# A chunked attention head pair: values and row sums from one product [V | 1] on half the rows of the array

## The chip, the cores and the metric

The kernel runs on one core of a Trainium2 chip. Times are device microseconds (us) of an execution. The kernel before takes 293.57 us (median of 4 executions beside the changed kernel, 292.65 to 294.11).

Engine names in the profile: PE is TensorE (matmuls), PEld its weight loads, DVE is VectorE, ACT is ScalarE, POOL is GpSimd, SP is SyncE, which issues transfers.

## The reference

Attention inside chunks of 64 tokens, then a two-layer network with a leaky ReLU (slope 0.01) on all 4608 tokens:

```python
# q, k, v: (8, 8, 576, 64) = batch, heads, tokens, head size
scores = scale * q_c @ k_c.T            # 64 x 64 in each chunk
attn   = exp(scores - max) ; attn /= sum(attn)
out    = attn @ v_c
x      = out as (4608 tokens, 512)
h      = x @ w_in                       # 512 -> 2048
y      = max(0.01 * h, h) @ w_out       # 2048 -> 512
```

## The kernel before

The kernel works in nine blocks (j) of 512 tokens. While TensorE does the network of block j, the attention of block j+1 is threaded between its steps. Two heads form a pair (kk), with one head in partitions 0 to 63 and the other in 64 to 127; a block has four pairs, so there are 36 pairs in all. Each pair passes four stages:

```python
def attn_t(j, kk, n=0):      # keys into a block-diagonal tile kd, 64 rows each
    ...
    for hh in range(2):
        ...
        if hh == 0 and (j == 0 and kk < 3 or j >= NPT and n >= NFC):
            nc.scalar.activation(out=dst, in_=src, func=AFT.Copy, ...)
        else:
            nc.vector.tensor_copy(out=dst, in_=src)     # the "kd copies"

def attn_s(j, kk):           # scores: 8 matmuls of 64 columns, then e = exp
    ...
def attn_x(j, kk):
    e = live[j, kk]
    zp = psum([128, TB], FP32, "zp", "at")
    nc.tensor.matmul(out=zp, lhsT=onesd, rhs=e, start=True, stop=True)   # sums
    xp = psum([128, R, 128], FP32, "xp", "at")
    for c in range(NC):                                                  # values
        nc.tensor.matmul(out=xp[:, :, c * NI:(c + 1) * NI],
                         lhsT=VD[j % NVD][:, kk, c, :, :],    # block diagonal, zeros off it
                         rhs=e[:, :, c * NI:(c + 1) * NI], start=True, stop=True)
    rz = sbuf([128, TB], FP32, "rz", 2)
    nc.scalar.activation(out=rz, in_=zp, func=AFT.Ln, ...)
    nc.scalar.activation(out=rz, in_=rz, func=AFT.Exp, ..., scale=-1.0)  # 1/sum
    live[j, kk] = (xp, rz)

def attn_n(j, kk):           # the "multiply"
    ...
    nc.vector.tensor_tensor(out=xT[j][:, kk, :], in0=xp..., in1=rz, op=ALU.mult)
```

The loop of block j has 32 steps n: 16 for the first layer (`hp`, four accumulating matmuls each, one per pair of xT), then the second (`mp`, sums of products with w_out, which VectorE combines). From block 3 on, pair kk does `attn_t` at step 7kk, `attn_s` at 7kk+3, `attn_x` at 7kk+5 and `attn_n` at 7kk+7. So step 7 holds the multiply of pair 0 **and** the kd copies of pair 1, and the loop issues the later stage first:

```python
def regular(first, gap, lags=(0, 3, 5, 7)):
    return [[first + gap * kk + lag for kk in range(NKK)] for lag in lags]
...
for s in (3, 2, 1, 0):                       # attn_n before attn_x, attn_s, attn_t
    for kk in range(NKK):
        at.setdefault(steps[s][kk], []).append((STEPS[s], kk))
```

PSUM, the memory that matmuls write into, has four banks for attention tiles (`at`) and four for the network (`mm`).

The softmax here doesn't subtract the row's maximum and nothing guards it: scores larger than these inputs give would overflow.

Of the kernel before, what the change touches and what calls it, by code (L numbers as in the profile page):

```python
# [9 lines left out]
FP32 = mybir.dt.float32  # L10
ALU = mybir.AluOpType
AFT = mybir.ActivationFunctionType
# [3 lines left out]
def kernel(  # L16
# [9 lines left out]
    nc = tc.nc  # L26
# [5 lines left out]
    CH = 64  # L32
    NKK = H // 2
    NFC = d_ff // 128
    TB = 512
    NJ = n_tok // TB
    NC = TB // CH
    R = 4
    NI = CH // R
# [11 lines left out]
    onesd = sb.tile([128, 128], FP16, name="onesd")  # L51
# [9 lines left out]
    NVD = 2  # L61
    KD = [sb.tile([128, NC, 2, CH], FP16, name=f"kd{m}") for m in range(NKD)]
    VD = [sb.tile([128, NKK, NC, 2, CH], FP16, name=f"vd{m}") for m in range(NVD)]
# [1 line left out]
        nc.vector.memset(t[0:64, :, 1, :], 0.0)  # L65
        nc.vector.memset(t[64:128, :, 0, :], 0.0)

    def clear_vd(m, eng):
        eng.memset(VD[m][0:64, :, :, 1, :], 0.0)
        eng.memset(VD[m][64:128, :, :, 0, :], 0.0)  # L70

    clear_vd(0, nc.vector)

    w_in = sb.tile([128, NKK, d_ff], FP16, name="w_in")
    w_out = sb.tile([128, NFC, d_model], FP16, name="w_out")
# [20 lines left out]
    def sbuf(shape, dtype, name, bufs):  # L96
        return sb.tile(shape, dtype, name=name, tag=name, bufs=bufs)

    def psum(shape, dtype, name, tag):
        return ps.tile(shape, dtype, name=name, tag=tag, bufs=4)  # L100


    def alloc(j):
        raw[j] = (
            sbuf([128, H, R * D], FP32, "qf", 2),
            sbuf([128, H, R * D], FP32, "kf", 2),
            sbuf([128, len(HW), NC, D], FP32, "vf", 2),
        )
        half[j] = tuple(sbuf([128, NKK, R, 2, D], FP16, n, 2) for n in ("qh", "kh"))
# [109 lines left out]

    def attn_x(j, kk):  # L220

        e = live[j, kk]
        zp = psum([128, TB], FP32, "zp", "at")
        nc.tensor.matmul(out=zp, lhsT=onesd, rhs=e, start=True, stop=True)  # L224
        xp = psum([128, R, 128], FP32, "xp", "at")
        for c in range(NC):
            nc.tensor.matmul(  # L227
                out=xp[:, :, c * NI:(c + 1) * NI],
                lhsT=VD[j % NVD][:, kk, c, :, :],
                rhs=e[:, :, c * NI:(c + 1) * NI],  # L230
                start=True,
                stop=True,
            )
        rz = sbuf([128, TB], FP32, "rz", 2)
        nc.scalar.activation(out=rz, in_=zp, func=AFT.Ln, bias=0.0, scale=1.0)  # L235
        nc.scalar.activation(out=rz, in_=rz, func=AFT.Exp, bias=0.0, scale=-1.0)  # L236
        live[j, kk] = (xp, rz)

    def attn_n(j, kk):

        if j not in xT:
            xT[j] = sbuf([128, NKK, TB], FP16, "xT", 2)
        xp, rz = live.pop((j, kk))
        nc.vector.tensor_tensor(  # L244
            out=xT[j][:, kk, :], in0=xp.rearrange("p r t -> p (r t)"), in1=rz, op=ALU.mult
        )

    STEPS = (attn_t, attn_s, attn_x, attn_n)

    def mm1_part(j, hp, fc, kk):  # L250
# [8 lines left out]
    def mm1_end(j, hp, fc):  # L259
        if fc == 0:  # L260
            gT[j] = sbuf([128, NFC, TB], FP16, "gT", 1)
        nc.scalar.activation(  # L262
            out=gT[j][:, fc, :], in_=hp, func=AFT.Prelu, bias=0.0, scale=1.0, alpha=0.01
        )
# [144 lines left out]
    with tc.manual_schedule():  # L409
# [9 lines left out]
        for step in range(NKK + 2):  # L419
            if step < NKK:  # L420
                if step == 3:
                    w_dma.append(load_w_in(0))
                cast_qk(1, 0, step, nc.gpsimd)
                cast_qk(0, 0, step, nc.gpsimd if step else nc.vector)
                if step == 3:
                    cast_v(0, 2)
                    w_dma.append(load_w_in(1))
                    cast_v(0, 3)
                    w_dma += [load_w_in(g) for g in range(2, 4)]
            p = step - 2  # L430
            if 0 <= p < NKK:
                attn_x(0, p)
            p = step - 1
            if 0 <= p < NKK:
                attn_s(0, p)
            if step < NKK:
                attn_t(0, step)
            p = step - 2
            if 0 <= p < NKK:
                attn_n(0, p)  # L440
            if step < NKK:
                keep_warm(3)
# [3 lines left out]
                mm1_part(0, hp, fc, kk)  # L446
        for fc, hp in enumerate(hps):
            mm1_end(0, hp, fc)
        clear_vd(1, nc.vector)
        alloc(1)  # L450
        for kk in range(NKK):
            first = load_qk(1, 2 * kk, 2 * kk + 2)[0]
# [23 lines left out]
        for j in range(NJ):  # L476
# [16 lines left out]
            for n in range(2 * NFC + (16 if j == 0 else 0)):  # L493
# [29 lines left out]
                if j + 2 < NJ:  # L523
                    if n in range(cast_at, cast_at + 8, 2):
                        kk = (n - cast_at) // 2
# [41 lines left out]
```

## Time and profile before

The profile on hand:

```profile
span 1162.2 us, 5938 instructions
PE 1155.9 (99%) x2264; PEld 471.7 (41%) x2264; DVE 192.7 (17%) x425; ACT 173.7 (15%) x295; POOL 100.5 (9%) x165
```

This page shows an execution four times as long as a timed one, so something was wrong with it. Its timeline (columns: start, duration in us, engine, source line, operation and count) shows what: a 512-column matmul starts 0.84 us before the next instruction.

```profile
505.88 1.16 PE L224 MATMUL zp<-e,onesd 128*128 128x512 f16 x1
506.72 1.16 PE L227 MATMUL xp<-e,vd_76 128*128 128x64 f16 x8
507.57 1.16 PE L333 MATMUL mp<-ws_b_22_85,a_22_1293 128*128 128x256 f16 x2
```

At that pace nearly every wait of TensorE for another engine disappears (two are left, of 1.5 and 0.7 us). The other engines ran at their usual speed. A second profile of the same kernel was taken later, as the first experiment (292.35 us, one execution, so its state is not labelled, but its time is that of the timed runs). It is the one to read against the kernel after:

```profile
span 290.6 us, 5938 instructions
PE 275.5 (95%) x2264; PEld 177.4 (61%) x2264; DVE 202.3 (70%) x425; ACT 166.5 (57%) x295; POOL 108.7 (37%) x165
PE 59%; DMA 19%; SPq 7%; DVE 7%; POOL 5%; issue 1%; ACT 0%; DVEq 0%; POOLq 0%
```

The last line is the chain of work that ended last, by engine (a q behind a name marks the engine's instruction sequencer). TensorE is busy for 95% of the span, and most of the chain is its own; what is not lies mainly in the start and the first blocks, where loads and the first heads' chains come in. From block 4 on the block starts are 28.77 us apart, and in that stretch the view of waits lists no wait of TensorE at all. VectorE is busy 70% of the time.

The groups that the change touches (line, engine, operation, shapes, count; busy us and mean ns; idle time before them and what ended it), at full clock:

```profile
L224 PE MATMUL zp<-e,onesd 128*128 128x512 f16 x36 | 13.6, 379 | 0.7 <-ACT e L217 0.7
L227 PE MATMUL xp<-e,vd 128*128 128x64 f16 x288 | 14.3, 193 | 0.4 <-DMA vd<-in_v_dram 0.4
L235 ACT ACTIVATE rz<-zp 128x512 f32<-128x512 f32 x36 | 21.4, 594 | 21.4 <-PE zp L224 20.1 <-DVE xT L244 1.2
L244 DVE TENSOR_TENSOR xT<-xp,rz 128x512 f16<-128x512 f32 x36 | 24.6, 686 | 22.6 <-ACT rz L236 20.6 <-PE op L277 1.6
L69 DVE MEMSET vd<- 64x1024 uint32 x2 | 1.8, 912 | 0.4 <-issue 0.2 <-DVE xT L244 0.2
```

A matmul's mean includes the run-out of the pipeline; from start to start a 512-column one takes 0.216 us here (median over hp). That is what the Trainium skill gives ("TensorE: Matmul & The Clock Gate", Part 1: 215.7 ns), so this trace agrees with the page.

### The profile page before, as it was taken

How to read it: one execution, taken by the hardware profiler on the slowest of the kernel's cores; microseconds unless marked ns; L12 is line 12 of the kernel's file. 1: busy time of each engine (PE TensorE's matmuls, PEld its weight loads, DVE VectorE, ACT ScalarE, POOL GpSimd, SP SyncE). 2: the span in 40 equal slices, each digit the busy share in tenths (PEclk: the TensorE clock that was granted, in tenths of full speed). 3: DMA queues.
4: the chain of work that ended last, by engine and by line, in shares of the span. 5: the costliest groups of instructions: out<-in, count | busy, mean ns of one | idle time of the engine just before them, and what ended most of it. 6: DMA issues, size and time to landing. Idle time of an engine off the chain costs nothing.

```text
span 1162.2 us, 5938 instructions
## 1 busy us (share of the span) xinstructions
PE 1155.9 (99%) x2264; PEld 471.7 (41%) x2264; DVE 192.7 (17%) x425; ACT 173.7 (15%) x295; POOL 100.5 (9%) x165
## 2 busy tenths in 40 slices
PE   9999999999999999999999999999999999999998
PEld 4523333322335523543354345334533543454244
DVE  2200111020121212221112111120212111111111
ACT  1211100101111112202211221122022112211110
POOL 5600002101000020120002001200100000000000
DMA  9950000133000024226005300700220010000000
GB/s 207 220 88 0 1 0 0 10 82 81 0 1 0 19 45 86 41 53 119 1 18 96 58 1 18 154 0 1 37 45 0 1 37 0 0 19 19 0 0 37
DMA packets 92605, 46.28 MB, mean 40 GB/s; under 512 B 65440, under 2 KB 87968, under 8 KB 92576
## 3 DMA queue, kind: packets, MB, share of 16 engines
q1 hardware_dynamic: 68896, 39.33, 14.6%
q0 software_dynamic: 23680, 6.56, 5.4%
q8 instruction: 18, 0.29, 0.1%
q14 instruction: 11, 0.09, 0.0%
HBM read 36.70 MB, written 9.44 MB: 40 GB/s over the span
## 4 chain that ended last, share of the span: by engine, by line
PE 99%; DVE 0%; ACT 0%; issue 0%
PE hp L251 46%; PE mp L333 32%; PE op L277 7%; PE xp L227 3%; PE sp L209 3%; PE zp L224 3%; PE warm L396 2%; PE tp L185 2%; PE tk L185 0%; ACT e L217 0%; DVE osb L298 0%; DVE wz L56 0%; DVE onesd L54 0%; DVE onesd L52 0%; DVE onesd L53 0%
## 5 line engine op out<-in xcount | busy, mean ns | idle before, releaser
L251 PE MATMUL hp<-xT,w_in 128*128 128x512 f16 x576 | 546.5, 1241 | 0.0
L251 PEld LDWEIGHTS <-w_in 128*128 128x128 f16 x576 | 136.0, 239 | 349.5 <-issue 349.1
L262 ACT ACTIVATE gT<-hp 128x512 f16<-128x512 f32 x144 | 86.0, 597 | 550.8 <-PE hp L251 550.8
L333 PEld LDWEIGHTS <-gT 128*128 128x128 f16 x512 | 112.9, 222 | 104.1 <-issue 104.1
L333 PE MATMUL mp<-w_out,gT 128*128 128x256 f16 x256 | 117.6, 696 | 0.0
L277 PE MATMUL op<-w_out,gT 128*128 128x512 f16 x64 | 87.7, 1700 | 0.0
L333 PE MATMUL mp<-ws_b_11_87,gT 128*128 128x256 f16 x128 | 59.8, 734 | 0.0
L333 PE MATMUL mp<-ws_b_12_86,gT 128*128 128x256 f16 x128 | 57.3, 725 | 0.0
L244 DVE TENSOR_TENSOR xT<-xp,rz 128x512 f16<-128x512 f32 x36 | 24.7, 686 | 160.4 <-ACT rz L236 142.3
L224 PE MATMUL zp<-e,onesd 128*128 128x512 f16 x36 | 44.8, 1245 | 0.7 <-ACT e L217 0.7
L217 ACT ACTIVATE e<-sp 128x512 f16<-128x512 f32 x36 | 21.5, 597 | 148.6 <-PE sp L209 148.6
L235 ACT ACTIVATE rz<-zp 128x512 f32<-128x512 f32 x36 | 21.5, 597 | 136.7 <-PE zp L224 129.4
L189 DVE COPY qt<-tp 128x512 f16<-128x512 f16 x12 | 5.1, 424 | 206.9 <-PE tp L185 206.9
L277 PEld LDWEIGHTS <-gT 128*128 128x128 f16 x64 | 19.2, 308 | 48.3 <-issue 48.1
L165 POOL CAST vd_75<-vf 64x512 f16<-64x512 f32 x20 | 12.6, 630 | 290.4 <-PE xp L227 152.3
L227 PEld LDWEIGHTS <-vd_75 128*128 128x128 f16 x160 | 24.2, 203 | 24.7 <-issue 22.6
L156 POOL CAST kh<-kf 128x512 f16<-128x512 f32 x36 | 21.9, 624 | 133.9 <-DMA kf<-in_k_dram 133.0
L396 PE MATMUL warm<-wz,onesd 128*128 128x512 f16 x20 | 27.9, 1694 | 1.5 <-DVE onesd L54 1.5
L209 PEld LDWEIGHTS <-kd_73 128*128 128x128 f16 x144 | 21.5, 201 | 17.5 <-issue 15.9
L227 PEld LDWEIGHTS <-vd_76 128*128 128x128 f16 x128 | 19.5, 204 | 19.4 <-issue 19.4
L227 PE MATMUL xp<-e,vd_75 128*128 128x64 f16 x160 | 26.0, 386 | 0.0
L209 PEld LDWEIGHTS <-kd_74 128*128 128x128 f16 x144 | 21.6, 204 | 10.2 <-issue 10.2
(287 smaller groups left out, 690.2 us busy)
## 6 DMA issues: line engine op xcount, KB each, us to landing
out_dram<-osb SPq DMA_DIRECT2D x36, 256.0 KB, 2.5
w_in<-in_moe_w_in_dram POOLq DMA_DIRECT2D x4, 512.0 KB, 8.0
w_out<-in_moe_w_out_dram POOLq DMA_DIRECT2D x4, 512.0 KB, 13.0
qf<-in_q_dram SPq DMA_DIRECT2D x4, 384.0 KB, 7.5
kf<-in_k_dram SPq DMA_DIRECT2D x4, 384.0 KB, 10.5
qf<-in_q_dram SPq DMA_DIRECT2D x5, 256.0 KB, 6.0
kf<-in_k_dram SPq DMA_DIRECT2D x5, 256.0 KB, 6.4
qf<-in_q_dram SPq DMA_DIRECT2D x2, 640.0 KB, 9.7
```

Source lines behind the costliest of these rows:

```text
L156: eng.tensor_copy(out=half[j][a][:, kk, :, :, :], in_=raw[j][a][:, 2 * kk:2 * kk + 2, :].rearrange("p h (r d) -> p r h d", r=R),)
L185: nc.tensor.transpose(out=t[:, a, r, :], in_=half[j][a][:, kk, r, :, :], identity=ident)
L209: nc.tensor.matmul(out=sp[:, :, c * NI:(c + 1) * NI], lhsT=kd[:, c, :, :], rhs=qt[:, :, c * NI:(c + 1) * NI], start=True, stop=True,)
L217: nc.scalar.activation(out=e, in_=sp, func=AFT.Exp, bias=0.0, scale=SCL)
L224: nc.tensor.matmul(out=zp, lhsT=onesd, rhs=e, start=True, stop=True)
L227: nc.tensor.matmul(out=xp[:, :, c * NI:(c + 1) * NI], lhsT=VD[j % NVD][:, kk, c, :, :], rhs=e[:, :, c * NI:(c + 1) * NI], start=True, stop ...
L244: nc.vector.tensor_tensor(out=xT[j][:, kk, :], in0=xp.rearrange("p r t -> p (r t)"), in1=rz, op=ALU.mult)
L251: nc.tensor.matmul(out=hp, lhsT=w_in[:, kk, fc * 128:(fc + 1) * 128], rhs=xT[j][:, kk, :], start=(kk == 0), stop=(kk == NKK - 1),)
L262: nc.scalar.activation(out=gT[j][:, fc, :], in_=hp, func=AFT.Prelu, bias=0.0, scale=1.0, alpha=0.01)
L277: nc.tensor.matmul(out=o, lhsT=gT[j][:, fc, ti * 128:(ti + 1) * 128], rhs=w_out[:, fc, :], start=(fc == 0), stop=(fc == NFC - 1),)
L333: nc.tensor.matmul(out=o, lhsT=a[:, i, u * 128:(u + 1) * 128], rhs=b[:, i, :], start=(i == 0), stop=(i == NH - 1),)
L396: nc.tensor.matmul(out=warm, lhsT=onesd, rhs=wz, start=True, stop=True)
```

## The change

The intent: the ones product streams 512 columns for each pair (0.216 us, 36 times, 7.8 us) only to add up rows. The tile VD has a free half beside each head's values. Fill it with ones instead of zeros, and one product per head over its own 64 rows gives values and sums together. Two heads then sit one above the other on the array, in different rows, and may run at the same time.

```diff
-    def clear_vd(m, eng):
-        eng.memset(VD[m][0:64, :, :, 1, :], 0.0)
-        eng.memset(VD[m][64:128, :, :, 0, :], 0.0)
+    def ones_vd(m, eng):
+        eng.memset(VD[m][0:64, :, :, 1, :], 1.0)
+        eng.memset(VD[m][64:128, :, :, 0, :], 1.0)
...
     def attn_x(j, kk):
         e = live[j, kk]
-        zp = psum([128, TB], FP32, "zp", "at")
-        nc.tensor.matmul(out=zp, lhsT=onesd, rhs=e, start=True, stop=True)
-        xp = psum([128, R, 128], FP32, "xp", "at")
+        xs = [psum([128, R, 128], FP32, n, "at") for n in ("xa", "xb")]
         for c in range(NC):
-            nc.tensor.matmul( ... lhsT=VD[j % NVD][:, kk, c, :, :], ... )
+            for hh, x in enumerate(xs):
+                rows = slice(hh * CH, (hh + 1) * CH)
+                nc.tensor.matmul(
+                    out=x[:, :, c * NI:(c + 1) * NI],
+                    lhsT=VD[j % NVD][rows, kk, c, :, :],
+                    rhs=e[rows, :, c * NI:(c + 1) * NI], start=True, stop=True)
-        nc.scalar.activation(out=rz, in_=zp, func=AFT.Ln, ...)
+        for hh, x in enumerate(xs):
+            nc.scalar.activation(out=rz[hh * CH:(hh + 1) * CH, :],
+                in_=x[(1 - hh) * CH:(2 - hh) * CH, :, :]..., func=AFT.Ln, ...)
...
     def attn_n(j, kk):
-        nc.vector.tensor_tensor(out=xT[j][:, kk, :], in0=xp..., in1=rz, op=ALU.mult)
+        for hh, x in enumerate(xs):
+            rows = slice(hh * CH, (hh + 1) * CH)
+            nc.vector.tensor_tensor(out=xT[j][rows, kk, :],
+                in0=x[rows, :, :]..., in1=rz[rows, :], op=ALU.mult)
```

So, for each pair: on TensorE 16 matmuls of 64 rows in place of one and 8 of 128 rows; on ScalarE two Ln in place of one; on VectorE two multiplies in place of one, because values and sums of the two heads now lie in different banks.

More of the change, by code (lines that the diff above doesn't have):

```diff
@@ L66 @@
         nc.vector.memset(t[64:128, :, 0, :], 0.0)
-    def clear_vd(m, eng):
-        eng.memset(VD[m][0:64, :, :, 1, :], 0.0)
-        eng.memset(VD[m][64:128, :, :, 0, :], 0.0)
-    clear_vd(0, nc.vector)
+    def ones_vd(m, eng):
+        eng.memset(VD[m][0:64, :, :, 1, :], 1.0)
+        eng.memset(VD[m][64:128, :, :, 0, :], 1.0)
+    ones_vd(0, nc.vector)
     w_in = sb.tile([128, NKK, d_ff], FP16, name="w_in")
@@ L222, in attn_x @@
         e = live[j, kk]
-        zp = psum([128, TB], FP32, "zp", "at")
-        nc.tensor.matmul(out=zp, lhsT=onesd, rhs=e, start=True, stop=True)
-        xp = psum([128, R, 128], FP32, "xp", "at")
+        xs = [psum([128, R, 128], FP32, n, "at") for n in ("xa", "xb")]
         for c in range(NC):
-            nc.tensor.matmul(
-                out=xp[:, :, c * NI:(c + 1) * NI],
-                lhsT=VD[j % NVD][:, kk, c, :, :],
-                rhs=e[:, :, c * NI:(c + 1) * NI],
-                start=True,
-                stop=True,
-            )
-        rz = sbuf([128, TB], FP32, "rz", 2)
-        nc.scalar.activation(out=rz, in_=zp, func=AFT.Ln, bias=0.0, scale=1.0)
+            for hh, x in enumerate(xs):
[3 more added lines that the diff above has]
+                    lhsT=VD[j % NVD][rows, kk, c, :, :],
+                    rhs=e[rows, :, c * NI:(c + 1) * NI],
+                    start=True,
+                    stop=True,
+                )
+        rz = sbuf([128, TB], FP32, "rz", 2)
+        for hh, x in enumerate(xs):
+            nc.scalar.activation(
+                out=rz[hh * CH:(hh + 1) * CH, :],
+                in_=x[(1 - hh) * CH:(2 - hh) * CH, :, :].rearrange("p r t -> p (r t)"),
+                func=AFT.Ln, bias=0.0, scale=1.0,
+            )
         nc.scalar.activation(out=rz, in_=rz, func=AFT.Exp, bias=0.0, scale=-1.0)
-        live[j, kk] = (xp, rz)
+        live[j, kk] = (xs, rz)
     def attn_n(j, kk):
@@ L242, in attn_n @@
             xT[j] = sbuf([128, NKK, TB], FP16, "xT", 2)
-        xp, rz = live.pop((j, kk))
-        nc.vector.tensor_tensor(
-            out=xT[j][:, kk, :], in0=xp.rearrange("p r t -> p (r t)"), in1=rz, op=ALU.mult
-        )
+        xs, rz = live.pop((j, kk))
+        for hh, x in enumerate(xs):
+            rows = slice(hh * CH, (hh + 1) * CH)
+            nc.vector.tensor_tensor(
+                out=xT[j][rows, kk, :],
+                in0=x[rows, :, :].rearrange("p r t -> p (r t)"),
+                in1=rz[rows, :],
+                op=ALU.mult,
+            )
     STEPS = (attn_t, attn_s, attn_x, attn_n)
@@ L448 @@
             mm1_end(0, hp, fc)
-        clear_vd(1, nc.vector)
+        ones_vd(1, nc.vector)
         alloc(1)
```

## The prediction

It was written with the slow profile as the only trace.

> **What bounds the kernel now.** TensorE, but the profiled execution is not a timed one: its span is 1162.2 us, the timed runs take 293.35. The busy table and the chain of waits both have PE at 99%. There a 128x512 matmul starts every 0.84 us (timeline, about 505 us) and every 1.28 us early on. I use it for order and the other engines' durations. By the groups the 2264 matmuls stream 634,880 columns (scores, ones and values 18,432 each). At 215.7 ns per 512 columns (the Trainium skill, "TensorE: Matmul & The Clock Gate", Part 1; no trace here shows it) that is 267 us by estimate, 91% of 293.35. The rest is mostly the start.
>
> **Removed.** 36 ones products of 512 columns: 7.8 us at that rate.
>
> **Added.**
> - TensorE: 16 loads and 16 matmuls of 64 columns and 64 rows in place of 8 and 8 per head pair. If the two halves overlap fully, the net is -7.8 us; if not at all, 0. The Trainium skill ("TensorEngine Tiling (Array Packing)", Key Properties) says that changing the tiling mode drains TensorE. Each head pair enters and leaves the half-row mode; I put 0.1 to 0.2 us on each switch (estimate): 72 switches, +7 to +14 us. I expect poor overlap at 64 columns: net +2 us (-7 to +12).
> - ScalarE: two Ln of 64x512 for one of 128x512. Partitions don't shorten an instruction (64x512 copies take as long as 128x512 ones), so +0.60 us each, 36 times.
> - VectorE: two multiplies for one, +0.69 us each.
> Neither becomes the limit: from 600 to 727 us (one block of 512 tokens) VectorE works about 22 us and ScalarE 19, of about 29 in a timed run.
>
> **Critical path.** The latency counts. Ones first let Ln begin while the values ran. Now the chain from the last values matmul is Ln, Ln, Exp, multiply, multiply: about 3.4 us with hand-overs, where it was 2.0. In steady blocks the fourth pair's values are at step 26; between them and the first hp matmul that needs its xT stand three w_out products (3 x 0.88 us) and three hp matmuls (0.65): 3.3 us by estimate. So I expect about 0.5 us of TensorE wait at each of 8 boundaries: +4 us. At the start the same chain stands before the fourth accumulation step: +1.5 us. In the first block the pairs stand one step apart, and both of a pair's banks (of four) are now held until the multiply: +1.5 us.
>
> **Sum.** 293.35 + 2 + 4 + 1.5 + 1.5 = 302.4; waits may overlap, so 300.5. Range 291 to 310. Faster by over 2%: 0.09; within 2%: 0.36; slower by over 2%: 0.55.
>
> **What would show it.** Groups: Ln 72 times at 0.60, multiplies 72 at 0.69, no ones product. Waits: hp matmuls waiting for the second multiply at block starts, in a trace at full clock; in a slow one they vanish. Timeline: the first-to-last start of a values section, and the gap to the next matmul, tell overlap and drain. If the profile after is as slow, a section that took 1.7 us there (ones plus values) should be near 1.7 plus drains without overlap, 0.85 plus drains with it; its span may then fall although the timed runs don't.
>
> **What would make it wrong.** Halves that overlap fully with cheap switches: about 287 to 292 us. Drains of 0.3 us or more: over 310. Slack at the block boundaries: 4 us less.

## The result, and the profile after

The changed kernel is correct and takes 314.37 us (median of 4, 314.09 to 315.74): 1.072 times the kernel before (95% interval 1.068 to 1.076). Ratios in this document are the mean time of one kernel's fast runs over that of the other's in the same rounds, so not quite the ratio of the medians. "Adds" below means this ratio less one, times 293.6 us. The change adds 21 us; 7 were predicted, and 310 was the upper end of the range.

The page of the kernel after, at full clock but for three short stretches named below (span, busy times, chain that ended last by engine):

```profile
span 312.3 us, 6496 instructions
PE 283.6 (91%) x2516; PEld 174.9 (56%) x2516; DVE 223.7 (72%) x461; ACT 188.2 (60%) x331; POOL 103.3 (33%) x165
PE 55%; DVE 29%; ACT 8%; issue 6%; DVEq 0%
```

VectorE's share of the chain went from 7% to 29%, while its share of busy time went only from 70% to 72%. The groups:

```profile
L237 ACT ACTIVATE rz<-xa 64x512 f32<-64x512 f32 x36 | 21.4, 593 | 22.0 <-PE xb L228 21.4
L237 ACT ACTIVATE rz<-xb 64x512 f32<-64x512 f32 x36 | 21.2, 589 | 0.9
L252 DVE TENSOR_TENSOR xT<-xa,rz 64x512 f16<-64x512 f32 x36 | 24.4, 678 | 26.9 <-ACT rz L242 26.6
L252 DVE TENSOR_TENSOR xT<-xb,rz 64x512 f16<-64x512 f32 x36 | 25.0, 695 | 0.8
L69 DVE MEMSET vd_75<- 64x2048 f16 x1 | 1.8, 1765 | 0.5 <-issue 0.5
```

Half the partitions do not shorten an instruction: each half costs what the whole did. And a memset of ones takes 1.77 us where one of zeros took 0.91.

**TensorE's part.** Here is one pair in a steady block of the kernel before, with the next scores:

```profile
157.36 0.38 PE L224 MATMUL zp<-e,onesd 128*128 128x512 f16 x1
157.58 0.40 PE L227 MATMUL xp<-e,vd 128*128 128x64 f16 x8
157.81 2.75 PE L251 MATMUL hp<-xT,w_in 128*128 128x512 f16 x12
160.40 1.04 PE L333 MATMUL mp<-w_out,gT 128*128 128x256 f16 x8
161.28 1.04 PE L333 MATMUL mp<-ws_b,gT 128*128 128x256 f16 x8
162.15 0.40 PE L209 MATMUL sp<-qT,kd 128*128 128x64 f16 x8
```

And the same place in the kernel after (the brackets give idle time and what ended it):

```profile
169.02 1.89 PE L262 MATMUL hp<-xT,w_in 128*128 128x512 f16 x8
170.85 0.20 PE L228 MATMUL xa<-e,vd_76 64*128 64x64 f16 x1
170.85 0.20 PE L228 MATMUL xb<-e,vd_76 64*128 64x64 f16 x1
170.88 0.19 PE L228 MATMUL xa<-e,vd_76 64*128 64x64 f16 x1
170.89 0.19 PE L228 MATMUL xb<-e,vd_76 64*128 64x64 f16 x1
...
171.06 0.19 PE L228 MATMUL xb<-e,vd_76 64*128 64x64 f16 x1
171.19 2.76 PE L262 MATMUL hp<-xT,w_in 128*128 128x512 f16 x12
173.79 1.04 PE L344 MATMUL mp<-w_out,gT 128*128 128x256 f16 x8
174.66 1.04 PE L344 MATMUL mp<-ws_b_11_87,gT 128*128 128x256 f16 x8
176.26 0.41 PE L209 MATMUL sp<-qT,kd_73 128*128 128x64 f16 x8 [0.57 <-DVE kd_73 L201]
```

The halves of a pair start within 0.01 us of each other, and the next two 0.03 us later: they overlap fully. But the eight hp matmuls from 169.02 would, at 0.2157 us each, have let the first half start at 170.75, and it started at 170.85; and from there to the hp matmul at 171.19 it is 0.12 us more than the 0.22 us that the columns stream. So entering and leaving the half-row mode costs 0.10 and 0.12 us, in each of the 20 pairs from block 3 on, and that eats the 0.22 us that the ones product took: 0.45 us from 157.36 to 157.81 before, 0.44 us from 170.75 to 171.19 after. The records of the weight loads show what differs. Before, the load for the values starts within 0.01 us of the start of the ones product (157.36), so it runs beneath it. After, the first half-row load starts at 170.84, 0.31 us after the start of the hp matmul before it, and so only when that has streamed.

**The stop.** The last line shows a new wait: the scores wait for kd. The kernel before has none there. VectorE's timeline at this place, before:

```profile
158.50 0.75 DVE L298 TENSOR_TENSOR gT<-gT 128x512 f16<-128x512 f16 x2
159.35 0.69 DVE L244 TENSOR_TENSOR xT<-xp,rz 128x512 f16<-128x512 f32 x1
159.96 1.20 DVE L201 COPY kd<-kT 64x512 f16<-64x512 f16 x2
```

and after:

```profile
172.78 0.75 DVE L309 TENSOR_TENSOR gT<-gT 128x512 f16<-128x512 f16 x2
173.56 0.68 DVE L252 TENSOR_TENSOR xT<-xa,rz 64x512 f16<-64x512 f32 x1
174.28 0.69 DVE L252 TENSOR_TENSOR xT<-xb,rz 64x512 f16<-64x512 f32 x1
175.00 1.21 DVE L201 COPY kd_73<-kT 64x512 f16<-64x512 f16 x2
```

Count from the end of the pair's section on TensorE (157.81 and 171.19). The scores are due 4.34 us after it (162.15 before; after, the mp matmuls of 174.66 end their streaming at 175.53). Before, the kd copies end 3.35 us after it: 0.99 us of slack. After, they end 5.02 us after it: 0.68 us late. The kd copies have nothing to do with the pair's multiplies; they only stand behind them in VectorE's queue.

A steady block has three such places. From the traces of blocks 4 to 6: before, the scores there have 0.95, 0.99 and 0.26 to 0.43 us of slack; after, they are 0.68, 0.73 and 0.30 to 0.49 us late. One more multiply of 0.69 us would not use up the first two. But the delays add up. In block 5 of the kernel before, VectorE has idle gaps of only 0.17 us in all in the 10.4 us from the first pair's multiply on; in the same block after, it has none over 0.05 us for 12.8 us. What one pair's second multiply adds is still in the queue when the next pair's comes.

Lines of the view of waits for scores and hp (who waited for whom: us in total, times, longest), before:

```profile
PE sp L209 <- DVE kd L201: 5.3, 7, 1.8
PE hp L251 <- DVE xT L244: 0.2, 1, 0.2
```

and after:

```profile
PE sp L209 <- DVE kd_73 L201: 4.7, 8, 0.9
PE hp L262 <- DVE xT L252: 4.4, 8, 1.6
PE sp L209 <- DVE kd_74 L201: 3.7, 8, 0.7
```

Such a list counts from the modelled end of the last matmul, so it leaves out the run-out of the pipeline. A full account comes from the start times of all matmuls: what each interval exceeds the columns' streaming time (0.2157 us for 512; two half-row matmuls side by side count as one) is lost. From these two traces, in us, up to the start of block 3 and from there:

| | before, up to block 3 | after, up to block 3 | before, rest | after, rest |
|---|---|---|---|---|
| streaming | 99.2 | 95.8 | 168.1 | 163.8 |
| lost before scores | 5.0 | 7.2 | 2.3 | 9.5 |
| lost before hp | 0.7 | 4.4 | 0.1 | 3.1 |
| lost around and in values (and ones) | 1.8 | 8.0 | 0.3 | 4.4 |
| other losses | 6.3 | 9.0 | 1.0 | 1.1 |
| all lost | 13.8 | 28.6 | 3.6 | 18.1 |

Streaming falls by 7.7 us, as intended, and losses rise by 29.3. In the steady part the 4.4 us around the values are nearly all mode switches; before scores and before hp it loses 10.2 us that the kernel before does not.

Not all of the 28.6 us is waiting. The trace's record of the granted clock shows half of full speed in three stretches of the kernel after (9.0 to 15.8, 22.7 to 26.1 and 56.8 to 60.2 us); before, it is full from 5.0 us on. The hp matmuls from 22.7 us start 0.43 us apart. The matmuls that start in these stretches stream 6.5 us at full clock, so by estimate at most 6.5 us of the 28.6 is clock. Over the four timed runs of the kernel after, the mean clock (0.971 to 0.992) does not go with the time: the lowest took 314.57 us and the highest 314.17.

### The profile page after: what moved, and what is told of

Same layout as the page of the kernel before. It is cut to its first block, busy times and chain, and to the rows that moved or that the text cites. A ratio compares the mean times of both kernels' runs of the same rounds, so it can differ in the third digit from the quotient of the medians.

```text
span 312.3 us, 6496 instructions
## 1 busy us (share of the span) xinstructions
PE 283.6 (91%) x2516; PEld 174.9 (56%) x2516; DVE 223.7 (72%) x461; ACT 188.2 (60%) x331; POOL 103.3 (33%) x165
## 4 chain that ended last, share of the span: by engine, by line
PE 55%; DVE 29%; ACT 8%; issue 6%; DVEq 0%
PE hp L262 25%; PE mp L344 19%; DVE xT L252 10%; PE op L288 5%; ACT rz L237 4%; DVE gT L309 4%; DVE kd_73 L201 3%; PE sp L209 2%; DVE kd_74 L201 2%; PE xa L228 2%; DVE osb L309 2%; ACT rz L242 2%; PE tp L185 2%; ACT gT L273 1%; ACT e L217 1%
## 5 line engine op out<-in xcount | busy, mean ns | idle before, releaser
L262 PE MATMUL hp<-xT,w_in 128*128 128x512 f16 x576 | 133.6, 383 | 4.4 <-DVE xT L252 4.4
L262 PEld LDWEIGHTS <-w_in 128*128 128x128 f16 x576 | 54.7, 99 | 66.9 <-issue 8.8
L344 PEld LDWEIGHTS <-gT 128*128 128x128 f16 x512 | 49.2, 98 | 7.9 <-ACT gT L273 0.5
L252 DVE TENSOR_TENSOR xT<-xa,rz 64x512 f16<-64x512 f32 x36 | 24.4, 678 | 26.9 <-ACT rz L242 26.6
L344 PE MATMUL mp<-w_out,gT 128*128 128x256 f16 x256 | 33.2, 273 | 0.0
L252 DVE TENSOR_TENSOR xT<-xb,rz 64x512 f16<-64x512 f32 x36 | 25.0, 695 | 0.8
L309 DVE TENSOR_TENSOR gT<-gT 128x512 f16<-128x512 f16 (+1 forms) x52 | 24.8, 518 | 0.0
L242 ACT ACTIVATE rz<-rz 128x512 f32<-128x512 f32 x36 | 22.7, 630 | 1.1
L137 POOL DMA_DIRECT2D vd_76<-in_v_dram x32 | 21.6, 689 | 1.7 <-DMA w_out<-in_moe_w_out_dram 1.7
L237 ACT ACTIVATE rz<-xb 64x512 f32<-64x512 f32 x36 | 21.2, 589 | 0.9
L137 POOL DMA_DIRECT2D vd_75<-in_v_dram x32 | 21.6, 697 | 0.3 <-issue 0.3
L344 PE MATMUL mp<-ws_b_11_87,gT 128*128 128x256 f16 x128 | 16.8, 273 | 0.1
L344 PE MATMUL mp<-ws_b_12_86,gT 128*128 128x256 f16 x128 | 16.6, 273 | 0.0
L288 PE MATMUL op<-w_out,gT 128*128 128x512 f16 x64 | 16.6, 404 | 0.0
L165 POOL CAST vd_76<-vf 64x512 f16<-64x512 f32 x16 | 9.9, 617 | 14.6 <-DMA vf<-in_v_dram 10.2
```

The lines of the kernel that those rows point to most:

```text
L137: eng.dma_start(out=dst, in_=v[b, h, s:s + n, :].rearrange("(c p) d -> p c d", p=CH))
L237: nc.scalar.activation(out=rz[hh * CH:(hh + 1) * CH, :], in_=x[(1 - hh) * CH:(2 - hh) * CH, :, :].rearrange("p r t -> p (r t)"), func=AFT. ...
L242: nc.scalar.activation(out=rz, in_=rz, func=AFT.Exp, bias=0.0, scale=-1.0)
L252: nc.vector.tensor_tensor(out=xT[j][rows, kk, :], in0=x[rows, :, :].rearrange("p r t -> p (r t)"), in1=rz[rows, :], op=ALU.mult,)
L262: nc.tensor.matmul(out=hp, lhsT=w_in[:, kk, fc * 128:(fc + 1) * 128], rhs=xT[j][:, kk, :], start=(kk == 0), stop=(kk == NKK - 1),)
L288: nc.tensor.matmul(out=o, lhsT=gT[j][:, fc, ti * 128:(ti + 1) * 128], rhs=w_out[:, fc, :], start=(fc == 0), stop=(fc == NFC - 1),)
```

## The experiments

Two theories. **T, the queue theory:** TensorE now stops for VectorE, because the longer chain (Ln, Ln, Exp, multiply, multiply) stands in front of the kd copies and of the next block's first hp sum. **R, the array theory:** entering and leaving the half-row mode costs the time. Twelve kernels were run; all but two are correct.

### The kernel before again, for a profile

> The kernel before, unchanged, for a profile at full clock, since the one on hand was taken at about a quarter of it. Both theories: span about 291 us. The waiting theory (T: PE now waits for VectorE and ScalarE, because the chain from the values to xT is longer and sits in front of the kd copies): score matmuls wait for kd at most 1 us in all (after: 8.4 us on PE's own list), hp matmuls wait for xT under 1 us (after: 4.4). The array theory (R: entering and leaving the half-row mode costs the time, about 0.29 us at each of 72 switches): the section ones plus values takes about 0.45 us here, against 0.44 us from last to next neighbour in the kernel after; R needs it to be 0.2 us or less here.

Its span is 290.6 us; its lines are shown above. The section of ones and values takes 0.45 us against 0.44, and hp waits for xT 0.2 us in all, as T has it. T was wrong in one number: the scores do wait for kd, 5.3 us in 7 stops, but all in the start and the first blocks, none from block 4 on. R in its size (0.29 us for each switch) is already contradicted by the 0.10 and 0.12 us read above.

### The array's part alone

```diff
-        for hh, x in enumerate(xs): ... two Ln of 64x512
+        nc.scalar.activation(out=rz, in_=xs[1]..., func=AFT.Ln, bias=1.0, scale=0.0)
-        for hh, x in enumerate(xs): ... two multiplies of 64x512
+        nc.vector.tensor_tensor(out=xT[j][:, kk, :], in0=xs[0]..., in1=rz, op=ALU.mult)
```

> The array's part alone: [V | 1] in two halves as in the kernel after, but one Ln of 128x512 (of 0*x + 1, so the result is wrong on purpose) and one multiply of 128x512. T: 290 to 296 us, since neither ScalarE nor VectorE has more to do. R: about 314 us, as after.

Measured: 294.9 us (293.32 to 295.37), ratio 1.0039 (1.0004 to 1.0074): it adds 1.1 us, in which the slower memsets of ones are contained. The block period is 28.76 us (28.77 before). R is refuted, and the array's part has no gain to give either.

### All but the array

```diff
-        nc.tensor.matmul(out=zp, lhsT=onesd, rhs=e, ...)      # before the values
         for c in range(NC): ...
+        nc.tensor.matmul(out=zp, lhsT=onesd, rhs=e, ...)      # behind them
+        two Ln of 64 rows in attn_x, two multiplies of 64 rows in attn_n
```

> All but the array: the kernel before with its ones product moved behind the values, Ln in two halves, multiply in two halves; result right. T: 308 to 317 us, most of the loss. R: 293 to 297 us.

Measured: 311.59 us, ratio 1.0614 (1.0590 to 1.0638), as T has it: it adds 18.0 of the 21 us with the array in full-row mode as before. The two parts alone make 19.1 of 21.2 us; the other 2 us, about the width of the intervals, no run accounts for.

### One part at a time

The multiply alone in two halves:

```diff
-        nc.vector.tensor_tensor(out=xT[j][:, kk, :], in0=xp..., in1=rz, ...)
+        for rows in (slice(0, CH), slice(CH, 2 * CH)):
+            nc.vector.tensor_tensor(out=xT[j][rows, kk, :], in0=xp[rows]..., in1=rz[rows, :], ...)
```

> The kernel before with the multiply alone in two halves (VectorE +0.69 us each pair). T: 296 to 301 us, since the second multiply delays the kd copies by 0.7 us. R: 293 to 295 us.

Measured: 306.66 us, ratio 1.0453 (1.0428 to 1.0477). It adds 13.3 us where 2.5 to 7.5 were expected. The place was right, the size was not: the delays of several pairs add up. This is VectorE at the place shown above, with ScalarE's last step towards 1/sum (the pair's section on TensorE ends at 165.68):

```profile
166.55 0.63 ACT L236 ACTIVATE rz<-rz 128x512 f32<-128x512 f32 x1
167.19 0.75 DVE L302 TENSOR_TENSOR gT<-gT 128x512 f16<-128x512 f16 x2
167.96 1.39 DVE L245 TENSOR_TENSOR xT<-xp,rz 64x512 f16<-64x512 f32 x2
169.38 1.20 DVE L201 COPY kd<-kT 64x512 f16<-64x512 f16 x2
```

1/sum is ready at 167.18, but the multiplies start only at 167.96, when the queue comes to them; before, 1/sum was ready at 159.31 and the multiply started at 159.35. The kd copies end 4.90 us after the section, 1.55 us later than before, where one multiply is 0.69. For the pair before this one the delay is 0.82 us.

Ln alone in two halves (`rz[rows, :]` from `zp[rows, :]`):

> The kernel before with Ln alone in two halves (ScalarE +0.59 us each pair, multiply whole, ones first). Queue theory: it lengthens the same chain by 0.6 us where the multiply in two halves lengthened it by 0.7, but the multiply often waits behind other VectorE work anyway, so 294 to 301 us. If total ScalarE work mattered it would be no less than the 306.7 of the split multiply.

Measured: 295.76 us, ratio 1.0078 (1.0024 to 1.0132): 2.3 us. Both lengthen the same chain, by 0.59 and 0.69 us, and one costs nearly six times the other. The traces show why in the steady block: with Ln in two halves the kd copies are 0.6 us later at the first two of the three places, once each and not added up, and that is inside their slack of 0.95 and 0.99 us. The block takes 28.77 us as before; what is lost is lost before block 4. A second multiply is different: it is itself in VectorE's queue, and its delay stays there. That the multiply waits for other VectorE work anyway, as the expectation had it, is not what the trace shows at the place above: it starts 0.04 us after 1/sum.

The ones product behind the values, alone:

> The kernel before with its ones product moved behind the values and nothing else: the sums are ready about 0.23 us later. Queue theory: between 293.5 and 296.5 us, less than Ln in two halves (295.8), since the delay is shorter.

Measured: 293.21 us, ratio 0.9972 (0.9927 to 1.0016): no effect. Its median lies 0.3 us under the expected interval.

Both Ln and the multiply in two halves:

> The kernel before with both Ln and the multiply in two halves, ones still first. If the costs add on one chain: 293.5 + 2.2 (Ln alone) + 13.1 (multiply alone), 308 to 310 us; and the move of the ones behind the values, which the all-but-the-array kernel has besides (311.6), would be worth 2 to 3 us more. If they hide in each other: 306.5 to 307.5.

Measured: 310.33 us, ratio 1.0567 (1.0536 to 1.0597): 16.6 us, against 15.6 for the two apart. The costs add; the microsecond more is within the intervals. The median lies 0.3 us above the first expected range, and the ones moved behind besides (all but the array) are worth 1.3 us more, not 2 to 3.

### The order in VectorE's queue

```diff
-                for s in (3, 2, 1, 0):
+                for s in (0, 3, 2, 1) if j + 1 >= NPT else (3, 2, 1, 0):
```

The kd copies are issued before the multiplies where both stand in one step. No work is added or removed. In the kernel after:

> The kernel after, with one change of order: where a step holds both, the kd copies (for the next scores) are issued before the two multiplies (blocks 3 and later, whose keys come transposed by the DMA). Queue theory (the kd copies stand behind the multiplies in VectorE's queue, and the scores wait for them): the scores' stops, 1.7 us of TensorE time in each block of 512 tokens of the profile after, go; six or seven blocks have the new order, so 302 to 306 us, block period 29.1 to 29.5 us (30.9 after, 28.8 before). Rival (VectorE simply has too much work in all): the order changes nothing, 312 to 315 us.

Measured: 305.78 us (ratio 1.0432, 1.0390 to 1.0475), as expected, and 8.6 us less than the kernel after; the block period is 29.33 us at the end (29.5 to 29.8 earlier, partly above the expected range; two blocks there also have a stop of a w_out product for VectorE, 0.5 us in all). The rival, too much work in all whatever the order, is out. In a window of one steady block the list of waits has one line left, the block boundary:

```profile
PE hp L262 <- DVE xT L252: 0.3, 1, 0.3
```

The same reordering on the kernel with only the multiply in two halves:

> The kernel before with the multiply in two halves (306.7 us) and the same change of order. Queue theory: the scores' stops, 0.93 us in a block, go: 299 to 303 us. Rival: 305 to 308 us.

Measured: 302.49 us, ratio 1.0300 (1.0245 to 1.0355), 4.2 us less than without it, within the range given.

### The memset

```diff
-        eng.memset(VD[m][0:64, :, :, 1, :], 1.0)
+        eng.memset(VD[m][0:64, :, :, 1, :].bitcast(FP32), two)    # bits 0x3C003C00; the other half alike
```

> The kernel after, with its ones written as 64x1024 words of two ones instead of 64x2048 fp16 elements. The profile after shows 1.77 us for each such memset where the zeros of the kernel before took 0.91, and two stand before the first cast on VectorE; the first transpose came at 7.9 us, not 5.8. If that start is on the critical path to the end: 311.5 to 313 us (2 us less). If the start is bound by the loads: 314.

Measured: 312.02 us, ratio 1.0641 (1.0568 to 1.0715) against 1.0721: 2.3 us less. The intervals of the two ratios touch, so the time alone is weak; but in the trace block 0 starts at 20.7 us instead of 22.7, as the two memsets have it.

### Does the overlap need the alternation?

```diff
-        for c in range(NC):
-            for hh, x in enumerate(xs):
+        for hh, x in enumerate(xs):
+            for c in range(NC):
```

on the kernel with the array's part alone:

> The array's part alone, but all eight matmuls of the first half before the eight of the second, where the array's part alone alternates them (294.9 us; result wrong on purpose as there). If the alternation is what lets the two halves run side by side, 16 matmuls of 64 columns now take 16 x 0.027 = 0.43 us in place of 0.22: +0.2 us for each of 36 pairs, 300 to 303 us. If the halves overlap however they are ordered: 294 to 296 us.

Measured: 296.95 us, ratio 1.0098 (1.0056 to 1.0140), between the two expectations. The trace shows why:

```profile
210.10 0.32 PE L228 MATMUL xa<-e,vd 64*128 64x64 f16 x5
210.24 0.20 PE L228 MATMUL xb<-e,vd 64*128 64x64 f16 x1
210.26 0.19 PE L228 MATMUL xa<-e,vd 64*128 64x64 f16 x1
210.28 0.19 PE L228 MATMUL xb<-e,vd 64*128 64x64 f16 x1
```

All eight xa stand before all eight xb in the program, yet the first xb starts before the sixth xa, in all 20 pairs from block 3 on. The second half overtakes, though only from the sixth on, and the block takes 29.28 us instead of 28.76: 0.13 us for each pair. The alternation is worth about that.

### The kernel after with three repairs

```diff
+ the order of VectorE's queue and the memset as above, and in blocks 3 and later the fourth pair earlier:
-            }.get(j, regular(0, 7))
+            }.get(j, [[0, 7, 14, 20], [3, 10, 17, 23], [5, 12, 19, 25], [7, 14, 21, 27]])
```

> The kernel after with three repairs: kd copies before the multiplies (305.8 us alone), ones written as words (2.3 us less alone), and in blocks 3 and later the fourth pair one step of the loop earlier, so that its chain ends before the next block's fourth accumulation step. The stop at the block boundary (0.46 us in each of six blocks in the profile of the reordered kernel) should go: 299 to 302 us, block period 28.8 to 29.1 us from block 4 on. It should not beat the kernel before: the array's part gains nothing by itself, and the stops of the start and of the first three blocks stay.

Measured: 302.24 us (ratio 1.0285), 0.2 us above the expected range; the period from block 4 on is 28.76 us at each block, exactly that of the array's part alone, and the list of waits of TensorE for two of those blocks is empty. In the steady blocks, then, the stops were the whole of the loss. What stays, about 8.4 us, lies in the start and the first three blocks: block 3 starts at 124.8 us, at 114.5 in the kernel before.

No kernel that was run is shown to be faster than the one before, and the runs say why: with all stops gone a steady block is as long as before (28.76 and 28.77 us). A gain would need fewer mode switches, for instance two pairs' values together; by estimate from the 0.22 us of a pair's two switches that is about 0.11 us a pair, 4 us in all, and it was not tried.

## Why the prediction was wrong

- **Slower, and through waits rather than work: right.** It put 0.55 on slower by over 2%. It is slower by 7.2%, outside the range.
- **"Neither becomes the limit": the step that failed.** By share of busy time it is true (72% for VectorE; in block 5 it works 24.3 of 30.9 us, before 20.9 of 28.8). But for 12.8 us of a steady block VectorE has no gap, so there it is the limit, and TensorE stops wherever one late instruction of that queue feeds it. The prediction followed the lengthened chain to its own consumer, xT, and did not ask who stands *behind* the multiplies. In three of four places of a steady block those are kd copies, and their scores had 0.95, 0.99 and 0.26 to 0.43 us of slack. The term is missing altogether: scores lose 7.2 us more in the steady part, and the reordering alone gave 8.6 us back.
- **"About 0.5 us of TensorE wait at each of 8 boundaries: +4 us": right in place, and in size for the steady blocks.** The stop there is 0.46 us by start times from block 4 on. The first three boundaries lose 1.72, 0.99 and 0.67 us, so that hp loses 6.7 us more than before in all (7.5 against 0.8), about 1.7 of them by estimate to the half clock from 22.7 us.
- **"I expect poor overlap at 64 columns: net +2 us": wrong on the overlap, small in sum.** The halves overlap fully (-7.8 us); the two switches cost 0.22 us a pair (7.9 us, near the lower end of the 7 to 14 given). The array's part alone adds 1.1 us including the memset. That the net came so close is luck in part: full overlap was not expected, and the 0.1 to 0.2 us a switch was a guess with no trace behind it.
- **The drain.** The Trainium skill ("TensorEngine Tiling (Array Packing)", Key Properties) says that changing the tiling mode drains TensorE. The trace agrees that a switch costs something, 0.10 us going in and 0.12 coming out, and that the first weight load behind it waits until the matmul before it has streamed; the page gives no figure.
- **Ln and multiply, +0.60 and +0.69 us each:** the durations were right (0.59 and 0.69). As terms of the time they were not alike: 2.3 and 13.3 us. In the steady block ScalarE's delay stays inside the slack of the kd copies; VectorE's delays add up in its queue.
- **The memset was not costed:** the prediction passed over 0.0 turning into 1.0. That is about 2.3 us, since two memsets stand before the first cast on VectorE. The Trainium skill would have told ("VectorE: DVE Perf Modes", "Zero memsets can be issued as uint32 (trn2)"): a memset takes a cycle per element whatever the type, and a zero of a narrow type can be issued at four bytes per element. The trace agrees that the number of elements decides: 64x1024 uint32 in 0.91 us, 64x2048 f16 in 1.77.
- **"At the start ... +1.5", "in the first block ... +1.5": too small together.** Of the 21.7 us between the two spans, 11.4 arise before block 3. Against the kernel before, 2 are the memsets, and all but the array already has 9.6 of them (block 3 at 124.1). The banks that are held until the multiply do cause stops (the waits of xa, xb, scores and transposes for xT sum to 5.0 us there), but all but the array, which holds no second bank, adds only 0.8 us less than the kernel after with its memset repaired. VectorE's queue has the largest part that single changes show: in the profiled executions, one of each kernel, block 4 starts at 145.2 us before, 148.5 with Ln in halves, 152.6 with the multiply in halves, 155.3 with all but the array and 157.5 after. How the rest divides between held banks and the half clock (at most 6.5 us by the estimate above) stays open.

Part of the miss may have come from the evidence: in a trace at a quarter of TensorE's pace a slack before a matmul looks about four times as long, and the prediction had to work out the slacks by hand. It did so for one consumer of three.

## What to carry to other kernels

When a change adds an instruction to an engine whose queue runs in order, as VectorE's does in these traces, list what stands behind it in that queue and who waits for that; the share of busy time does not show it, and a queue without gaps passes each delay on to the next addition. Moving independent work ahead of the addition can win back part of the loss without removing any work (8.6 of 21 us here). Splitting an instruction over partitions doubled its cost here (0.68 and 0.70 us for one of 0.69), so a layout that saves TensorE columns but puts two heads' results in two banks pays for it on the engines that read them. Matmuls on half the rows do run side by side, but each visit to that mode cost 0.22 us here, so by estimate a section gains from it only if it saves more streaming time than that; none that did was run.

## What the Trainium skill lacked or had wrong

- "TensorEngine Tiling (Array Packing)", Key Properties, says that a mode switch drains TensorE and gives no figure. Here a 128-row to 64-row switch costs 0.10 us and the way back 0.12, beyond streaming, in all steady pairs.
- "TensorE: Matmul & The Clock Gate", Part 3, says that matmuls are strictly in program order in start and end. With eight matmuls on one half of the rows before eight on the other, the trace has the first of the second half start before the sixth of the first (210.24 and 210.26 us). The starts are those of the trace's records; a rebuild of the kernel has all eight of the first half before the second in TensorE's instructions.
- The same page, Part 1, warns that the clock gate has been seen stuck at a quarter for over 50 us. Here a whole profiled execution of 1162 us ran at about that pace (0.84 us for 512 columns, against 0.216 at full clock) and slower still early on (1.28), with a mean granted clock of 1.00 in the records: the spacing of matmuls, not the recorded clock, showed it. Whether it was the clock gate is not shown.
